# Another order for the start of a Fourier-and-maxout kernel: transfers, weight conversions and early quads

## The chip, the cores and the metric

The kernel runs on one core of a Trainium2 chip. The metric is the device time of one execution in microseconds (us). Engines are named as in the profile: PE does the matmuls, DVE, ACT and POOL work on tiles, SP here only issues DMAs; ACT and POOL issue some as well.

## What is computed

x has the shape (8, 3072, 256), in float32. The reference, cut to what matters:

```python
X = np.fft.rfft(x, axis=1)
Yr = Xr @ w_r - Xi @ w_i + b_r
Yi = Xr @ w_i + Xi @ w_r + b_i
Yr = np.sign(Yr) * np.maximum(np.abs(Yr) - lam, 0.0)     # lam = 0.01, Yi likewise
y = np.fft.irfft(Y, n=3072, axis=1)
h = np.maximum(np.maximum(y @ w1, y @ w2), y @ w3)       # 24576 rows, 256 to 768
out = h @ w_out                                          # 768 to 256
```

The expert weights w1, w2, w3 and w_out arrive in float64.

## The kernel before

**The Fourier part** of one batch has two levels, because 3072 = 96 x 32. *Stage a* is a 96-point transform as matmuls into `pa`; it goes over 8 quads, each of 4 of the 32 columns. A quad loads x (`load_x`), takes the largest magnitudes `mxx` that later set the scale (batch 1 on), copies `pa` to `aq` on ACT (L465) and writes it to the DRAM tile `a_d` (L466). Then come 12 *groups*: a group k reads its rows `aj` of `a_d`, does the 64-point blocks into `px` (L524, tables `mb_f`), the products with w_r, w_i into `py` (L551, L552, weights `wst`), adds the bias (`uf`, L555), thresholds (ACT L557 and L558, DVE L559), takes the maximum `mxu` (L712) and goes back through `pz` (L567; the last group L570, table `qf`). ACT copies `pz` to `zs` (L731) and writes it to the DRAM tile `z_d` (L732). Batch 0 does this in plain float32, stage a of batch 1 too; later batches split every operand into two parts and use three matmuls (`mm3`, L159 to L161).

**The expert part** loops over batch b, chunk c (8 of 384 rows) and f (6 slices of 128 of the 768 columns): `load_z` reads `zq` from `z_d`, `split_z` makes `zh` on ACT and `zl` on DVE (L153, L154), `inverse` transforms into `pi` and splits to `yh`, `yl`; `up` does the three products `pu`, with their maximum on DVE (`c` L817, `h` L820); `down` does `pd`. Stage a and the groups of the next batches are woven in between by a list of `events`, each with a position in units of f.

**The prologue** is batch 0's Fourier part; no expert work runs beside it. Its loop (L911) runs k from -3 to 12 and hands out loads and weight work by `plan[k]`. With k=12 done, two quads of batch 1 run their stage a, then 16 matmuls on a tile of zeros (`idle_matmuls`, L867), then `load_z`, `split_z`, `inverse` and the first `up`. I call this stretch, from the last `pz` to the first `pu`, the *pause*: PE has to wait there for z_d to go to DRAM and back. There are 9 idle matmuls at the very start and 32 between stage a and the groups.

**The weights.** `Weights` converts a float64 block of 384 columns (up) or 256 (down) into two float16 parts with integer work on DVE and ACT, in three steps: `exponent` (DVE L352, ACT L355), `combine` (DVE L359, L362, L366, L367) and `finish` (ACT L126, DVE L127, L373); `largest` (L328) takes the maximum first. There are 12 up blocks and 6 down blocks. Six and three go through the groups by the plan; the rest are `units`, of which each call of `pump` moves every running one a step on and begins another. The maxima of w_r, w_i and of the bias (`mxc`, `mxb` L289), their exponents (a transposing matmul `pt`, L237) and the float16 parts of w_r and w_i come in `split_fft_weights`, called at b=c=0, f=2.

**What sets the order.** A scheduler orders the instructions of each engine; `issue_after` puts an instruction behind another in that order without a wait on the chip. Each engine issues its own DMAs in its own order. SP loads x, the tables, w_r, w_i, `aj`, the expert weights and `zq`; ACT writes `z_d`, and `a_d` from batch 1 on; POOL loads `qf`, the bias (`bias`, and one row of 1 KB more into partition 96, L225), the identity and `bias_ri`, and writes the eight quads of batch 0 to `a_d`.

Of the kernel before, what the change touches and what calls it, by code (L numbers as in the profile page):

```python
# [93 lines left out]
def fourier_maxout_kernel(  # L94
    ctx: ExitStack, tc: tile.TileContext, x, w_r, w_i, b_r, b_i, w1, w2, w3, w_out, fa, ga, mb, mq, ident, out
):
    nc = tc.nc
# [11 lines left out]
    NATIVE = 2 * NCH  # L109

# [35 lines left out]

    def split_later(hi, lo, src, scale=None):
        h = hi if hi.dtype == F16 else hi.bitcast(F32)
        if scale is None:
            nc.scalar.activation(out=hi, in_=src, func=AF.Copy)  # L150
            later(lambda: nc.vector.tensor_tensor(out=lo, in0=src, in1=h, op=ALU.subtract))
        else:
            nc.scalar.activation(out=hi, in_=src, func=AF.Copy, scale=scale)  # L153
            later(lambda: nc.vector.scalar_tensor_tensor(  # L154
                out=lo, in0=src, scalar=scale, in1=h, op0=ALU.mult, op1=ALU.subtract
            ))
# [44 lines left out]
    def x_tile(name):  # L201
        return fft.tile([P, 2 * D], F32, name=name, bufs=2)
# [9 lines left out]
    def load_fft_weights():  # L212
# [12 lines left out]
        nc.gpsimd.dma_start(out=bias[96:97, 1, :], in_=rows[0])  # L225
        return [ws[:, kd] for kd in range(KD)]

# [21 lines left out]
    def power(name, e, sign, add, bufs=3):  # L249
# [3 lines left out]
        nc.vector.tensor_scalar(out=t, in0=t, scalar1=23, scalar2=None, op0=ALU.logical_shift_left)  # L253
# [14 lines left out]
    def split_fft_weights(ws):  # L268
# [7 lines left out]
        sc = power("sc", e, -1.0, 267.0, 1)  # L276
# [10 lines left out]
        split_scaled(*(t.rearrange("p a b -> p (a b)") for t in (qh, ql, qf)), Q_SCALE)  # L287
# [11 lines left out]


# [6 lines left out]
    class Weights:  # L307
        def __init__(self, name, parts, both):
            self.name, self.parts, self.raw, self.both = name, parts, {}, both
            self.mx = fft.tile([P, len(parts)], F32, name="mw" + name, bufs=1)  # L310


        def load(self, n, homes=None):
            src = [self.parts[n + i][2] for i in range(2)]
            width = src[0].shape[1]
            if homes:
                for i, t in enumerate(homes):
                    raw = t.rearrange("p j d -> p (j d)").bitcast(U32)[:, 0:width]
                    nc.sync.dma_start(out=raw, in_=src[i])
                    self.raw[n + i] = raw.rearrange("p (v w) -> p v w", w=2)  # L320
                return
            raw = raw_tile("rw").bitcast(U32)[:, 0:2 * width].rearrange("p (k c) -> p k c", k=2)
            nc.sync.dma_start(out=raw, in_=self.both(n))
            for i in range(2):
                self.raw[n + i] = raw[:, i].rearrange("p (v w) -> p v w", w=2)

        def largest(self, n):
            nc.vector.tensor_reduce(  # L328
                out=self.mx[:, n:n + 1], in_=self.raw[n][:, :, 1].bitcast(F32), axis=AX.X, op=ALU.max,
                apply_absolute_value=True,  # L330
            )
# [9 lines left out]
        def phases(self, n):  # L341
            hi, lo, _ = self.parts[n]
            raw = self.raw[n]
            width = raw.shape[1]
            lw, hw = raw[:, :, 0], raw[:, :, 1]
# [3 lines left out]
            def exponent():  # L349
                e = x_tile("xh").bitcast(U32)[:, 0:width]  # L350
                t["g"] = g = x_tile("xl").bitcast(U32)[:, 0:width]
                nc.vector.tensor_scalar(  # L352
                    out=e, in0=hw, scalar1=0x7FF00000, scalar2=None, op0=ALU.bitwise_and
                )
                nc.scalar.activation(out=g, in_=e, func=AF.Relu, scale=8.0, bias=ebias)  # L355
# [27 lines left out]
        (wuh[:, i, kd, v:v + HALF], wul[:, i, kd, v:v + HALF],  # L383
         up_v[i][kd * P:(kd + 1) * P, 2 * v:2 * v + 2 * HALF])
        for v in range(0, FF, HALF) for i in range(3) for kd in range(KD)
    ], lambda n: up_v[n % 6 // 2][:, n // 6 * 2 * HALF:(n // 6 + 1) * 2 * HALF].rearrange(
        "(k p) w -> p k w", p=P
    ))
    w_dn = Weights("d", [
        (woh[:, f], wol[:, f], out_v2[f * P:(f + 1) * P]) for f in range(NF)  # L390
    ], lambda n: out_v2[n * P:(n + 2) * P].rearrange("(k p) w -> p k w", p=P))
# [19 lines left out]

    def batch(b, kind):
# [13 lines left out]
    def load_x(q):  # L426
        b, q4 = divmod(q, NCH)
        xv = x[b].rearrange("(n1 n2) d -> n1 n2 d", n2=N2)[:, q4 * NQ:(q4 + 1) * NQ, :]
        with tc.issue_after(st["ld"].ins) if q >= NCH + 2 else nullcontext():
            if 2 <= q < NCH:  # L430
# [6 lines left out]

    def split_x(q):
# [79 lines left out]
    def first_b(k):  # L518
# [17 lines left out]
        if k == NJP - 1:  # L536
            st["ts"] = s_tile("tsf").rearrange("p (h m) -> p h m", h=KD)
            nc.gpsimd.tensor_copy(out=st["ts"], in_=t[:, :, 192:320])
# [178 lines left out]
    def stage_q(k):  # L717
# [13 lines left out]
        nc.scalar.activation(out=zs, in_=pv, func=AF.Copy, scale=st[b, "sv"][1] if b else 1.0)  # L731
# [6 lines left out]
    events = []  # L738

    def at(pos, fn, i, k=None, n=None):  # L740
        if n is None or 0 <= k < n:
            events.append((pos, len(events), fn, i))

    for q in range(NCH + 2, NB * NCH):
# [15 lines left out]
    events.sort(key=lambda e: e[0:2])  # L760
# [98 lines left out]
    def load_first_blocks(i):  # L859
        k = slice(6 * i, 6 * i + 6)  # L860
        nc.sync.dma_start(out=mb_f[:, k], in_=mq[:, 2 + 6 * i:8 + 6 * i])
# [14 lines left out]
    load_first_blocks(0)  # L876
    fft_weights = load_fft_weights()
# [3 lines left out]
    idle_matmuls(32)  # L881
    nc.gpsimd.dma_start(out=id_sb, in_=ident)
# [21 lines left out]
    for n in range(6):  # L904
        planned((4, 4, 5, 5, 7, 7)[n], w_dn.largest, n)
    planned(7, w_dn.scale)
    for n in range(3):
        planned(5 + n, prepare, w_dn, n)
        planned(8 + n, phase, w_dn, n)

    for k in range(-3, NJP + 1):  # L911
# [108 lines left out]
```

## Time and profile before

| | |
|---|---|
| median of three runs | 2042.45 us (2041.36 to 2044.1) |
| profiled execution | 2041.44 us, of which the span of the trace is 2039.6 us |
| granted TensorE clock, mean | 0.998 |
| PE, DVE, ACT busy | 99%, 71%, 51% of the span |
| first `px` of group 0 | at 31.90 us |
| last `pz` of group 11 | at 101.39 us |
| first `pu` | at 112.68 us |

A row of a timeline gives the start, the duration, the engine with its line and the tiles (out<-in), and in brackets how long the engine had been idle and what released it. In a row of grouped instructions stand the count, the busy time and the mean in ns. A row of windows gives the busy time of PE, PE's weight loads, DVE, ACT and POOL, then the granted clock, the DMA engines' busy share and GB/s.

### The profile page before, as it was taken

The page shows a single profiled execution, that of the slowest core. Times are in us where ns is not written, and L with a number is a line of the kernel's source. Part 1 is how long each engine was busy: PE and PEld are TensorE (multiplying, and loading weights), DVE is VectorE, ACT ScalarE, POOL GpSimd, SP SyncE. Part 2 cuts the span into 40 slices and gives each one's busy share as a digit, 9 for nine tenths or more (in the row PEclk, how much of TensorE's full clock was granted, in tenths as well). Part 3 has the DMA queues.
Part 4 walks back from the last instruction along what each step waited for, and adds up shares of the span by engine and source line. Part 5 has one row for each costly group of instructions (what it writes and reads, how often), then busy time and mean ns, then how long its engine had stood idle before and what let it go on. Part 6 is the DMA issues. An engine that isn't in the chain of part 4 may idle for free.

```text
span 2039.6 us, 40089 instructions
## 1 busy us (share of the span) xinstructions
PE 2016.9 (99%) x15836; PEld 1413.9 (69%) x15836; DVE 1447.3 (71%) x2813; ACT 1032.3 (51%) x2050; POOL 24.3 (1%) x81
## 2 busy tenths in 40 slices
PE   8999999999999999999999999999999999999999
PEld 4756776677776777677776777767777677776666
DVE  3997886678766877668776777767876677755544
ACT  4756554455544554445554555545554455533333
POOL 1000000000000000000000000000000000000000
PEclk9999999999999999999999999999999999999999
DMA  9455542434333442434434344243441423211100
GB/s 312 149 160 140 141 119 86 119 99 124 93 103 84 120 115 72 125 80 123 105 95 113 81 120 104 80 117 98 109 111 47 117 73 100 66 53 32 40 24 24
DMA packets 199535, 207.74 MB, mean 102 GB/s; under 512 B 20131, under 2 KB 177827, under 8 KB 199251
## 3 DMA queue, kind: packets, MB, share of 16 engines
q1 hardware_dynamic: 138371, 129.20, 24.8%
q10 hardware_dynamic: 59744, 72.11, 11.1%
q0 software_dynamic: 1232, 3.87, 0.6%
q8 instruction: 124, 2.03, 0.4%
q14 instruction: 64, 0.52, 0.1%
HBM read 87.40 MB, written 75.50 MB: 80 GB/s over the span
## 4 chain that ended last, share of the span: by engine, by line
PE 89%; DMA 4%; DVE 4%; ACT 1%; issue 1%; SPq 0%; ACTq 0%; DVEq 0%
PE pu L159 17%; PE pu L160 17%; PE pu L161 17%; PE pd L161 6%; PE pd L160 6%; PE pd L159 6%; PE py L159 3%; PE py L161 3%; PE py L160 3%; PE px L586 2%; DMA ab<-a_d 1%; PE pa L161 1%; PE pa L160 1%; PE pa L159 1%; DMA zq<-z_d 1%; PE pi L161 1%
## 5 line engine op out<-in xcount | busy, mean ns | idle before, releaser
L159 PE MATMUL pu<-yh,wuh 128*128 128x384 f16 x2304 | 751.1, 326 | 6.0 <-ACT c L814 3.2
L160 PE MATMUL pu<-yl,wuh 128*128 128x384 f16 x2304 | 750.6, 326 | 0.9 <-DVE yl L154 0.7
L161 PE MATMUL pu<-yh,wul 128*128 128x384 f16 x2304 | 750.7, 326 | 0.0
L153 ACT ACTIVATE hh<-h 128x384 f16<-128x384 f32 x384 | 200.4, 522 | 530.8 <-DVE h L820 529.1
L817 DVE TENSOR_TENSOR c<-pu,c 128x384 f32<-128x384 f32 x384 | 211.9, 552 | 180.5 <-ACT c L814 93.7
L161 PEld LDWEIGHTS <-wul 128*128 128x128 f16 x2304 | 225.2, 98 | 150.9 <-issue 2.0
L159 PEld LDWEIGHTS <-wuh 128*128 128x128 f16 x2304 | 225.4, 98 | 130.5 <-issue 11.7
L160 PEld LDWEIGHTS <-wuh 128*128 128x128 f16 x2304 | 225.5, 98 | 130.0 <-issue 11.5
L161 PE MATMUL pd<-woh,hh 128*128 128x256 f16 x1152 | 313.7, 273 | 0.2 <-DVE ebf L294 0.2
L160 PE MATMUL pd<-wol,hh 128*128 128x256 f16 x1152 | 313.9, 273 | 0.0
L159 PE MATMUL pd<-woh,hh 128*128 128x256 f16 x1152 | 313.9, 273 | 0.0
L154 DVE SCALAR_TENSOR_TENSOR hh<-h,hh 128x384 f16<-128x384 f32 x384 | 213.1, 555 | 122.1 <-ACT hh L153 121.7
L814 ACT ACTIVATE c<-pu 128x384 f32<-128x384 f32 x384 | 185.8, 484 | 142.2 <-PE pu L161 123.4
L820 DVE TENSOR_TENSOR h<-pu,c 128x384 f32<-128x384 f32 x384 | 212.3, 553 | 57.9 <-PE pu L161 50.6
L159 PE MATMUL py<-wch,tt 128*128 128x256 f16 x504 | 137.4, 273 | 0.0
L161 PE MATMUL py<-wch,tt 128*128 128x256 f16 x504 | 137.3, 273 | 0.0
L160 PE MATMUL py<-wcl,tt 128*128 128x256 f16 x504 | 137.3, 272 | 0.0
L160 PEld LDWEIGHTS <-hh 128*128 128x128 f16 x1152 | 112.7, 98 | 33.4
L159 PEld LDWEIGHTS <-hh 128*128 128x128 f16 x1152 | 112.7, 98 | 33.4
L849 ACT ACTIVATE o<-pd,s1u 128x256 f32<-128x256 f32 x191 | 82.6, 466 | 82.2 <-PE pd L161 41.0
L161 PEld LDWEIGHTS <-hh 128*128 128x128 f16 x1152 | 112.7, 98 | 13.6 <-DVE ebf L294 0.5
L154 DVE SCALAR_TENSOR_TENSOR zl<-zq,s0u,zh 96x1024 f16<-96x1024 f32 (+1 forms) x65 | 81.9, 1262 | 31.8 <-ACT zh L153 31.8
(204 smaller groups left out, 2686.9 us busy)
## 6 DMA issues: line engine op xcount, KB each, us to landing
z_d<-zs ACTq DMA_DIRECT2D x96, 256.0 KB, 2.2
out_dram<-o ACTq DMA_DIRECT2D x190, 128.0 KB, 2.1
zq<-z_d SPq DMA_DIRECT2D x63, 384.0 KB, 4.1
xq<-in_x_dram SPq DMA_DIRECT2D x58, 384.0 KB, 4.1
a_d<-aq ACTq DMA_DIRECT2D x56, 384.0 KB, 3.3
ab<-a_d SPq DMA_DIRECT2D x84, 256.0 KB, 3.9
ab<-ab SPq DMA_DIRECT2D x336, 64.0 KB, 2.1
vb<-vb SPq DMA_DIRECT2D x308, 64.0 KB, 2.4
```

The source lines that it names most:

```text
L153: nc.scalar.activation(out=hi, in_=src, func=AF.Copy, scale=scale)
L154: later(lambda: nc.vector.scalar_tensor_tensor(out=lo, in0=src, scalar=scale, in1=h, op0=ALU.mult, op1=ALU.subtract))
L159: nc.tensor.matmul(o, lh, rh, start=start, stop=False, **kw)
L160: nc.tensor.matmul(o, lh, rl, start=False, stop=False, **kw)
L161: st["mm"] = nc.tensor.matmul(o, ll, rh, start=False, stop=stop, **kw)
L586: nc.tensor.matmul(pv[:, h, :, g // 2, g % 2], ah[:, g // 2, g % 2, h * P:(h + 1) * P], mb_sb[:, i, 4 * kb + g].rearrange("p (c m) -> p c ...
L814: nc.scalar.activation(out=c1, in_=p, func=AF.Copy)
L817: nc.vector.tensor_tensor(out=c1, in0=p, in1=c1, op=ALU.max)
L820: nc.vector.tensor_tensor(out=h32, in0=p, in1=st["c1"], op=ALU.max)
L849: nc.scalar.activation(out=o, in_=pd[t], func=AF.Copy, scale=st[b, "su"][1])
```

## The change

1. **Transfers.** POOL no longer loads `qf`, the bias and the identity ahead of the `a_d` writes: SP does, behind the first two `aj`, w_r and w_i. Only the 1 KB row is still POOL's, behind the writes, and `bias_ri` comes late. Of the first table block only a third is loaded ahead of `aj`, and the rest follows in pieces of 4 and 6. w_r and w_i are asked for in the loop at k=-3, and the expert weights one group later.
2. **Conversions.** Two up blocks (768 columns) or two down blocks (512) go through one instruction, apart from the down blocks 2 and 3. `exponent` works in place in one tile `xhl`.
3. **Held back.** From k=11 on, `pump` runs as `pumps`, behind `quiet`: first the power s1u of batch 0 on DVE and the last `zs` on ACT, later the last low part `zl` or `yl` on DVE. The x maxima of the early quads come later, by events.
4. **Early quads.** Five quads of batch 1 (8 to 12) run stage a in the pause instead of two. Their x is loaded at k=7 to 11, three of them into weight tiles. The idle matmuls become 34 (from 32) and 4 (from 16).
5. **Scales.** `scale_fft_weights` holds the maxima and exponents of w_r, w_i and the bias and runs at k=0; `split_fft_weights` keeps the rest, at f=2.

```diff
+    EARLY = NCH + 5
...
-        rows = [b.rearrange("(o d) -> o d", o=1) for b in (b_r, b_i)]
-        nc.gpsimd.dma_start(out=qf, in_=mq[:, 0:2])
-        for j in range(2):
-            for c in range(2):
-                nc.gpsimd.dma_start(
-                    out=bias[64 * c:64 * c + 64, j, :], in_=rows[c].broadcast_to([64, D])
-                )
-        nc.gpsimd.dma_start(out=bias[96:97, 1, :], in_=rows[0])
         return [ws[:, kd] for kd in range(KD)]
+
+    def load_tables():
+        rows = [b.rearrange("(r o d) -> r o d", r=1, o=1) for b in (b_r, b_i)]
+        for c in range(2):
+            nc.sync.dma_start(out=bias[64 * c:64 * c + 64], in_=rows[c].broadcast_to([64, 2, D]))
+        nc.gpsimd.dma_start(out=bias[96:97, 1:2], in_=rows[0])
+        nc.sync.dma_start(out=qf, in_=mq[:, 0:2])
+        nc.sync.dma_start(out=id_sb, in_=ident)
...
-            if 2 <= q < NCH:
+            if 2 <= q < NCH or NCH + 2 <= q < EARLY:
                 xq = raw_tile("xr")[0:N1, 0:NQ * D]
...
+    def largest_x(q, i, xp):
+        b, q4 = divmod(q, NCH)
+        with tc.issue_after(quiet[0]) if q < EARLY else nullcontext():
+            nc.vector.tensor_reduce(
...
+            if q >= EARLY:
+                largest_x(q, i, xp)
+            elif b:
+                at(1 + q4 / 2, lambda u: largest_x(*u), (q, i, xp))
...
-    idle_matmuls(32)
-    nc.gpsimd.dma_start(out=id_sb, in_=ident)
+    idle_matmuls(34)
...
-    for n in range(12):
-        if n % 2 == 0:
-            planned(-3 + n // 2, w_up.load, n)
+    for n in range(0, 12, 2):
+        planned(-2 + n // 2, w_up.load, n)
         planned(-2 + n // 2, w_up.largest, n)
-    for n in range(6):
-        planned(-1 + n, prepare, w_up, n)
+    for n in range(0, 6, 2):
+        planned(n, prepare, w_up, n)
         planned(5 + n // 2, phase, w_up, n)
...
         with tc.issue_after(st["ld"].ins):
+            if k == -3:
+                fft_weights = load_fft_weights()
+                load_first_blocks(2, 4)
+            if k == -2:
+                load_tables()
+            if k == 0:
+                scale_fft_weights(fft_weights)
...
-            if k in (7, 8):
+            if 7 <= k < 12:
                 load_x(NCH + k - 7)
             if k == 9:
-                units += [(w_up, n) for n in range(6, 12)] + [(w_dn, n) for n in range(3, 6)]
-            if k >= 9:
+                units += [(w_up, n) for n in (6, 8, 10)] + [(w_dn, n) for n in (3, 4)]
+            if k in (9, 10):
                 pump()
-    for q in (NCH, NCH + 1):
...
+    quiet = st["power"].ins, st["zs"].ins
+
+    def pumps(n):
+        with tc.issue_after(quiet[0]), tc.issue_after(quiet[1]):
+            for _ in range(n):
+                pump()
+
+    pumps(1)
+    for q in range(NCH, EARLY):
         split_x(q)
         stage_a(q)
-    idle_matmuls(16)
+    idle_matmuls(4)
...
+    quiet = st["low"].ins, st["zs"].ins
...
-                    for _ in range(5):
-                        pump()
+                    pumps(5)
                     if f == 2:
-                        split_fft_weights(fft_weights)
+                        with tc.issue_after(quiet[0]):
+                            split_fft_weights(fft_weights)
```

Where the order moves, at three places. First POOL at the start of the kernel, before:

```order
L219 DMA qf<-in_dft_ib_dram 128x256
L222 DMA bias<-in_b_r_dram 64x256
L222 DMA bias<-in_b_i_dram 64x256
L222 DMA bias<-in_b_r_dram 64x256
L222 DMA bias<-in_b_i_dram 64x256
L882 DMA id_sb<-in_ident_dram 128x128
L930 DMA bias_ri<-in_b_r_dram 128x256
L930 DMA bias_ri<-in_b_i_dram 128x256
L225 DMA bias<-in_b_r_dram 1x16x16
L466 DMA a_d<-aq 96x1024 x2
```

and after, where the eight quads lie in the tiles aq, zq, ga_sb and wuh, which are free at that time:

```order
L488 DMA a_d<-aq 96x1024 x2
L488 DMA a_d<-zq 96x1024
L488 DMA a_d<-ga_sb 96x1024 x3
L488 DMA a_d<-wuh 96x1024 x2
L228 DMA bias<-in_b_r_dram 1x16x16
L560 COPY tsf<-tf 128x256
L959 DMA bias_ri<-in_b_r_dram 128x256
```

Nine small loads stood ahead of the first a_d write; now none does, and the 1 KB row (1x16x16) stands behind the last.

Second, ACT in the pause, from the last `zs` on, before:

```order
L465 ACTIVATE aq<-pa 96x512
L466 DMA a_d<-aq 96x1024
L465 ACTIVATE aq<-pa 96x512
L126 ACTIVATE wuh<-rw,swu 128x384
L466 DMA a_d<-aq 96x1024
L355 ACTIVATE xl<-xh,ebias 128x384
L153 ACTIVATE zh<-zq,s0u 96x512 x2
L355 ACTIVATE xl<-xh,ebias 128x384
L153 ACTIVATE yh<-pi 128x384 x2
```

and after, where the first `aq` x2 is a half of each of the quads 8 and 9, and the others are both halves of one quad, 10, 11 and 12:

```order
L487 ACTIVATE aq<-pa 96x512 x2
L488 DMA a_d<-aq 96x1024 x2
L487 ACTIVATE aq<-pa 96x512 x2
L361 ACTIVATE xhl<-xhl,ebias 128x768
L488 DMA a_d<-aq 96x1024
L487 ACTIVATE aq<-pa 96x512 x2
L157 ACTIVATE zh<-zq,s0u 96x512
L488 DMA a_d<-aq 96x1024
L487 ACTIVATE aq<-pa 96x512 x2
L157 ACTIVATE zh<-zq,s0u 96x512
L488 DMA a_d<-aq 96x1024
L157 ACTIVATE yh<-pi 128x384 x2
```

Both halves of `zh` stood together behind two quads; now each half stands behind one or two quads more.

Third, DVE at the start of the groups, after (before, `mxc` and `mxb` stood ahead of all groups and their exponents `ec`, `eb` in the stretch from the pause to f=2):

```order
L277 TENSOR_REDUCE mxc<-wst 128x1 x2
L239 TENSOR_REDUCE col<-mxc 128x1
L128 SCALAR_TENSOR_TENSOR ql<-qf,qh 128x256
L577 TENSOR_TENSOR uf<-py,bias 128x512
L246 TENSOR_REDUCE ec<-pt 128x1
L284 TENSOR_REDUCE mxb<-bias 128x1
L247 TENSOR_SCALAR ec<-ec 128x1
L239 TENSOR_REDUCE col<-mxb 128x1
L250 TENSOR_SCALAR ec<-ec 128x1
```

`mxb`, which needs all of the bias with its 1 KB row, now stands behind the first `uf` and ahead of all later ones.

More of the change, by code (lines that the diff above doesn't have):

```diff
@@ L275, in split_fft_weights @@
         st["lim", "x"] = limits("x", e, 142.0)
-        sc = power("sc", e, -1.0, 267.0, 1)
+        st["sc"] = power("sc", e, -1.0, 267.0, 1)
+        mb = small("mxb")
+        nc.vector.tensor_reduce(
+            out=mb, in_=bias.rearrange("p j d -> p (j d)"), axis=AX.X, op=ALU.max,
+            apply_absolute_value=True,
+        )
+        st["eb"] = small("ebf")
+        nc.vector.tensor_scalar(
+            out=st["eb"], in0=exponent_of(mb, "b", 23, 0xFF, 60.0), scalar1=1.0, scalar2=-37.0,
+            op0=ALU.mult, op1=ALU.add,
+        )
+    def split_fft_weights(ws):
+        sc = st["sc"]
         for kd, t in enumerate(ws):
@@ L307, in fourier_maxout_kernel, with __init__ @@
     class Weights:
-        def __init__(self, name, parts, both):
-            self.name, self.parts, self.raw, self.both = name, parts, {}, both
+        def __init__(self, name, parts):
+            self.name, self.parts, self.raw = name, parts, {}
             self.mx = fft.tile([P, len(parts)], F32, name="mw" + name, bufs=1)
         def load(self, n, homes=None):
-            src = [self.parts[n + i][2] for i in range(2)]
-            width = src[0].shape[1]
+            width = 2 * self.parts[n][0].shape[1]
             if homes:
@@ L341, in phases @@
         def phases(self, n):
-            hi, lo, _ = self.parts[n]
             raw = self.raw[n]
-            width = raw.shape[1]
-            lw, hw = raw[:, :, 0], raw[:, :, 1]
+            pair, width = raw.shape[1:3]
+            if pair == 2:
+                hi, lo = self.parts[n][4]
+            else:
+                hi, lo = (t.rearrange("p (k c) -> p k c", k=1) for t in self.parts[n][0:2])
+            lw, hw = raw[:, :, :, 0], raw[:, :, :, 1]
             m, r = hw.bitcast(F32), lw.bitcast(F32)
@@ L349, in exponent @@
             def exponent():
-                e = x_tile("xh").bitcast(U32)[:, 0:width]
-                t["g"] = g = x_tile("xl").bitcast(U32)[:, 0:width]
+                g = x_tile().rearrange("p a b -> p (a b)")[:, 0:pair * width].bitcast(U32)
+                t["g"] = g = g.rearrange("p (k v) -> p k v", k=pair)
                 nc.vector.tensor_scalar(
-                    out=e, in0=hw, scalar1=0x7FF00000, scalar2=None, op0=ALU.bitwise_and
+                    out=g, in0=hw, scalar1=0x7FF00000, scalar2=None, op0=ALU.bitwise_and
                 )
-                nc.scalar.activation(out=g, in_=e, func=AF.Relu, scale=8.0, bias=ebias)
+                nc.scalar.activation(out=g, in_=g, func=AF.Relu, scale=8.0, bias=ebias)
             def combine():
@@ L436, in load_x @@
         st["x", q] = pairs
+    def largest_x(q, i, xp):
+        b, q4 = divmod(q, NCH)
+        with tc.issue_after(quiet[0]) if q < EARLY else nullcontext():
+            nc.vector.tensor_reduce(
+                out=batch(b, "x")[0:N1, 2 * q4 + i:2 * q4 + i + 1], in_=xp, axis=AX.X,
+                op=ALU.max, apply_absolute_value=True,
+            )
     def split_x(q):
@@ L537, in first_b @@
             st["ts"] = s_tile("tsf").rearrange("p (h m) -> p h m", h=KD)
-            nc.gpsimd.tensor_copy(out=st["ts"], in_=t[:, :, 192:320])
+            st["late"] = nc.gpsimd.tensor_copy(out=st["ts"], in_=t[:, :, 192:320])
             for z in (32, 96):
@@ L730, in stage_q @@
         zs = fft.tile([P, 2, D], F32, name="zs")
-        nc.scalar.activation(out=zs, in_=pv, func=AF.Copy, scale=st[b, "sv"][1] if b else 1.0)
+        st["zs"] = nc.scalar.activation(
+            out=zs, in_=pv, func=AF.Copy, scale=st[b, "sv"][1] if b else 1.0
+        )
         nc.scalar.dma_start(out=rows_of(b, "z", kb), in_=zs)
@@ L736, in stage_q @@
             st[b, "su"] = power("s0u", e, -1.0, 261.0), power("s1u", e, 1.0, add)
[L738 to L744, printed above, removed]
+    for q in range(EARLY, NB * NCH):
         b, i = divmod(q, NCH)
```

104 lines of the change are left out of this document (50 added, 54 removed).

## The prediction

> **What bounds the kernel now.** I read the page's totals first, then the PE timeline of the first 155 us, then the chain of waits in order of time, and last the timelines of POOL, DVE and ACT and the DMA issues.
>
> ```profile
> span 2039.6 us, 40089 instructions
> PE 2016.9 (99%) x15836; PEld 1413.9 (69%) x15836; DVE 1447.3 (71%) x2813; ACT 1032.3 (51%) x2050; POOL 24.3 (1%) x81
> ```
>
> PE fills 99% of the span, so the only time to be had lies where PE waits or runs the idle matmuls, which compute nothing. PE's timeline shows these places (start, duration; in brackets the idle time before and its releaser):
>
> ```profile
> 10.58 2.31 PE L462 MATMUL pa<-xr,fr 96*96 96x512 f32 x5
> 14.40 7.41 PE L462 MATMUL pa<-xr,fr 96*96 96x512 f32 x16 [1.51 <-DMA xr<-in_x_dram]
> 21.65 7.07 PE L870 MATMUL idle<-zeros 128*128 128x512 f16 x32
> 31.90 1.13 PE L524 MATMUL px<-mb_all,aj 128*128 128x128 f32 x8 [3.18 <-DMA aj<-a_d]
> ...
> 101.39 1.35 PE L570 MATMUL pz<-uf,qf 128*128 128x256 f32 x4 [1.66 <-DVE uf L559]
> 112.68 0.65 PE L159 MATMUL pu<-yh,wuh 128*128 128x384 f16 x3 [0.41 <-ACT yh L153]
> 153.66 0.33 PE L159 MATMUL pu<-yh,wuh 128*128 128x384 f16 x1
> ```
>
> I cut the start at these moments. px of group 0 starts at 31.90; E = 102.74 is the end of the last pz (101.39 and 1.35); P = 112.68 is the first pu; S = 153.66 is the first pu of chunk 1, f=2. From S on, PE's list is the same in both kernels, and up to S it has the same pu, pd and pa, so the change is worth what it moves S. The three pieces are 70.84 (group stage), 9.94 (pause) and 40.98 (first chunk).
>
> **The front, up to px of group 0.** The chain gives the last a_d write and the read behind it, and PE's pieces of the first groups; the POOL rows show who held the writes; the count of packets by queue from 15 to 17 us has SP's queue, q1, alone; the DMA issues up to 140 us give KB and median time to landing:
>
> ```profile
> 22.73 6.22 DMA a_d<-wuh
> 28.97 2.80 DMA aj<-a_d
> ...
> 34.79 0.85 PE py L552 x2
> 36.50 1.34 PE px L524 x8
> 37.84 0.43 PE py L552 x2
> 41.29 0.89 PE px L524 x8
> ```
> ```profile
> 11.96 0.52 POOL L225 DMA_DIRECT2D bias<-in_b_r_dram  x1 [6.19 <-DMA bias<-in_b_i_dram]
> 12.47 1.03 POOL L466 DMA_DIRECT2D a_d<-aq  x2
> ```
> ```profile
> q1 hardware_dynamic: 141, 0.48, 103.4%
> ```
> ```profile
> z_d<-zs ACTq DMA_DIRECT2D x12, 256.0 KB, 2.2
> ...
> a_d<-aq ACTq DMA_DIRECT2D x4, 384.0 KB, 3.8
> ...
> bias<-in_b_r_dram POOLq DMA_DIRECT2D x1, 1.0 KB, 7.7
> ```
>
> Before, POOL stood 6.19 us for its bias loads ahead of the a_d writes, and wst and the table blocks shared q1 with x. After, the writes stand first on POOL and x has q1 nearly alone. I let PE's 1.51 wait for x go (bounds 0 and 1.51), so the last a_d write is issued near 21.1 in place of 22.73. It no longer has a backlog of seven writes ahead, so I price it at the 3.8 us of the four later a_d writes; the other end is the 6.22 of its own row. aj is then asked for at 25.0 instead of 28.97 and px starts at 27.9: **-4.0** (bounds -1.5 and -4.6). The 34 idle matmuls, at 7.07/32 = 0.22 each, reach from 20.2 to 27.7 and cover the wait, so the 3.18 us hole closes as well.
>
> **The group stage, 70.84.** Step by step:
> - Behind the 3.18 us hole, the py pairs cost 1.08, 0.85 and 0.85 against 0.43, and px 1.34 against 0.89: a half-speed stretch of 0.65+0.42+0.42+0.45 = 1.9. Its clock stands in the window below (0.77 over 35 to 40). Without the hole: **-1.9** (bounds 0 and -1.9).
> - Two pt matmuls (the exponents of wst and bias), which ran in the pause, now run between py of groups 0 and 1. A pt pair on PE costs 0.44 to 0.68 by its rows below: **+0.55**.
> - Three pa matmuls instead of two stand ahead of the last pz, at 1.71/2 = 0.86 each: **+0.86**. They and a lighter DVE list cover most of the 1.66 wait for uf: **-1.35** (bounds -0.86 and -1.66).
> - The bias maximum mxb now stands early in DVE's list, between uf of group 0 and everything behind it, and PE's second pt waits for it. It needs the 1 KB row that POOL sends, which waits in turn for the bias loads that SP now issues behind aj, wst, a table block and a second aj, some 1.5 MB. At the 396 GB/s of the window from 35 to 40 below that is 3.8 us from 25.0, and with some 2.5 us until the last is through (an aj read alone took 2.80) they land near 31.3. Before, this row took 7.7 us (issue 11.96, mxb at 19.69) beside a full q1. PE reaches that pt at about 36.0 (first py at 29.75, 12 py at 0.43, px 0.89, pt 0.22). A row that lands at once costs nothing; one that takes 7.7 lands at 39.0 and holds PE until mxb's 0.69 and a column copy are through, 3.9. I take **+2.5**, nearer to the row. A half-speed stretch behind that wait (0 to 1.9) I leave out of the sum and keep in the range.
>
> ```profile
> 35.00:40.00 5.00, 5.00 (x23) 4.45 (x22) 3.46 (x9) 1.99 (x4) 0.00 (x0) 0.77 1.03 396
> ```
> ```profile
> 102.74 1.71 PE pa L462 x2
> 104.88 0.44 PE pt L237 x2
> ```
> ```profile
> 109.69 0.68 PE L237 MATMUL pt<-id_sb,col 128*128 128x128 f32 x4
> ```
> ```profile
> 19.69 0.69 DVE L289 TENSOR_REDUCE mxb<-bias 128x1 f32<-128x512 f32 x1 [11.60 <-DMA bias<-in_b_r_dram]
> ```
>
> The Trainium skill, "DMA: Bandwidth & Descriptors", section "Anatomy of one DMA — SWDGE (gpsimd) path", gives about 2.0 us fixed and little for 1 KB, and its section "Queues, rings and completion order" says that an engine takes its queues in turn, packet by packet. By that page the row would land near 33.3 and the +2.5 would be nothing. The 7.7 us row and the software queue without one packet from 15 to 17 speak against it.
>
> Sum of the stage: -1.9 + 0.55 + 0.86 - 1.35 + 2.5 = **+0.7**; E moves by -4.0 + 0.7 = -3.3.
>
> **The pause from E to P, 9.94.** Before, two quads of batch 1 had their stage a here and the chain ran over zs, its write, the read as zq, zh, zl, the inverse. After, five quads do. ACT is the engine to follow, because it copies pa into aq (two buffers), writes a_d and also makes zh:
>
> ```profile
> 103.41 0.37 ACTq L732 DMA_DIRECT2D z_d<-zs  x1
> 105.11 0.34 ACTq L466 DMA_DIRECT2D a_d<-aq  x1
> 107.12 0.66 ACT L126 ACTIVATE wuh<-rw,swu 128x384 f16<-128x384 f32 x1
> 108.75 1.32 ACT L153 ACTIVATE zh<-zq,s0u 96x512 f16<-96x512 f32 x2
> ```
> ```profile
> 110.29 1.41 DVE L154 SCALAR_TENSOR_TENSOR zl<-zq,s0u,zh 96x512 f16<-96x512 f32 x2
> ```
>
> In the new order of ACT, aq of the third quad stands ahead of the first zh, and aq of the fourth and fifth quads ahead of the first and second. Third and fourth wait for the first two buffers to be written out, the fifth for the third's write. From E: zs, a double-width wuh and two aq halves, 2.4; the write of the first quad, 3.8; two aq halves, 1.0; the write of the third, 3.8; two halves, 1.0; the second zh, 0.66; the second zl, 0.75; and from zl's end (111.70) to pu (112.68), 0.98. Sum 14.4: **+4.5**. Two a_d writes as quick as z_d's 2.2 would give 11.2, two like the 6.22 row 19.2; z's own path, at 9.94, is the floor. I take the 3.8 row, since it is the same transfer on the same queue. The conversions that DVE has ahead of zl, at the prices below 0.92 + 0.87 + 0.92 + 0.47 + 0.87 + 0.87 + 0.47 = 5.4 and with its scalar rows about 6.9, are done by E+7, in time; from there to E+13.4 DVE has only the two zl and stands about 5 us.
>
> **From P to S, 40.98.** Three quads' pa, six at 0.86, no longer stand here: -5.1. But DVE gets the conversions that were held back. One 768-wide conversion is priced from the 384- and 256-wide rows of 30 to 140 us (start to start 0.08 less than the mean):
>
> ```profile
> L127 DVE SCALAR_TENSOR_TENSOR rw<-rw,swu,wuh 128x384 f32<-128x384 f32 x12 | 7.2, 611 | 0.0
> ...
> L359 DVE SCALAR_TENSOR_TENSOR xl<-rw,xl 128x384 uint32<-128x384 uint32 x12 | 6.5, 551 | 0.4 <-ACT xl L355 0.4
> ...
> L127 DVE SCALAR_TENSOR_TENSOR rw<-rw,swd,woh 128x256 f32<-128x256 f32 x4 | 1.9, 477 | 0.0
> ...
> L359 DVE SCALAR_TENSOR_TENSOR xl<-rw,xl 128x256 uint32<-128x256 uint32 x4 | 1.7, 416 | 0.0
> ...
> L362 DVE TENSOR_SCALAR rw<-rw 128x384 uint32<-128x384 uint32 x12 | 4.2, 353 | 0.0
> ```
> ```profile
> 125.00:130.00 5.00, 5.00 (x38) 3.37 (x36) 5.00 (x22) 1.32 (x3) 0.00 (x0) 1.00 0.15 48
> ```
> ```profile
> 143.76 0.54 DVE L820 TENSOR_TENSOR h<-pu,c 128x384 f32<-128x384 f32 x1
> ```
>
> From 256 to 384 wide the L359 form grows by 0.135; three such steps more make 768 wide 0.47 + 0.40 = 0.87, against two of 384 at 0.94: pairing saves 8%. In the same way L127 gives 0.92, and L362, growing by 0.07, 0.47. DVE was full beside PE here (5.00 of 5 from 125 to 130). Adding up DVE's new list from P at these prices puts the last h of f=5 at P+34.4; before it ended at 144.2, P+31.5. So DVE is 2.9 later while PE has 5.1 less to do. Laid against PE's list, PE stands 2.0 at the pu of f=3, 2.8 at the pd behind f=1, and 0.55, 1.3 and 0.55 behind: 7.2 of waits, where the old list by the same count has 1.2. So +6.0 - 5.1 = **+0.9** (bounds -6.3, no wait at all, and +2.9, DVE's whole delay). Of the 16 idle matmuls of the pause 4 are left, and PE may enter f=0 at half speed, 1.9 at most as above; I cost that at nothing, as DVE is behind PE there, and at 1.9 if it is not.
>
> **Sum.** -4.0 + 0.7 + 4.5 + 0.9 = +2.1. Against the profiled execution's 2041.44 (span 2039.6 and 1.84 around it) that is 2043.5; the three runs' median, 2042.45, is 1.0 above it, so I forecast 2044.5 for the median. A change under 0.2%, 4.1 us, cannot be told from none by this measurement: faster means below 2038.4, slower above 2046.5.
>
> **The rivals.**
> - *DVE keeps up after P.* If pairing and holding back leave DVE less to do than my widened prices say, PE's waits don't grow and all of the 5.1 comes: P to S 6.0 better than forecast, 2038.5. For it: the 5 us in which DVE stands in the longer pause. Against it: the 5.00 of 5 row, and the conversions have not become fewer elements. If the 1 KB row comes at once too, 2036.0.
> - *The bias row is late.* It lands at 39.0 or later, as the 7.7 row says; PE waits 3.9 and a half-speed stretch of 1.9 follows, as after the hole of 3.18. That is 1.4 + 1.9 more: 2047.8. It decides from about 38 us on, when the wait is over twice the 1.66 us one. For it: DMA at 1.03 of 16 engines. The Trainium skill's "TensorE: Matmul & The Clock Gate", section "What's actually happening", asks for an idle window of about 3.4 us before the clock halves; by it a wait of 2.5 would cost no clock. The window from 100 to 105 below, with only a 1.66 us wait behind it, is at 0.72 and speaks against that.
>
> ```profile
> 100.00:105.00 5.00, 3.61 (x9) 2.03 (x10) 4.19 (x9) 2.86 (x6) 0.00 (x0) 0.72 0.49 155
> ```
>
> - *The early start runs into the transfers.* wst, bias, qf, identity and table blocks, some 1.5 MB, now pass between 25 and 35 us, where 396 GB/s is what the engines give. If py of group 0 or px of group 1 waits for them, the 3.3 is lost: 2047.8. Against it: the expert weights come one group later, which frees that much.
>
> - *The bias row is served at once.* If queues are served in turn, the row lands before PE asks for it, the 2.5 goes, and the rest stands: 2042.0, no change. For it: z_d, on a third queue, has a median of 2.2 over the same stages. Against it: the 7.7 row. The rule quoted from the page above says the same.
>
> **How the numbers follow.** Forecast: 0.40. DVE keeps up: 0.23, of which half lies under 2038.4, and more with the row at once. Row at once alone: 0.13. Late row: 0.16. Transfers: 0.08. A little of the forecast's own spread (the pause at its ends, -3.2 and +4.8) falls to each side. That makes faster 0.22, same 0.51, slower 0.27. The range, 2036.5 to 2049.5, reaches from the first rival with the row at once to the late row with a slower a_d write; the forecast's own is 2040.5 to 2047.
>
> **What would show it.** Right: px of group 0 near 27.9 with under 1 us of waiting before it; py pairs at 0.43 from the start; a PE wait of 1 to 4 us at the second pt, released by DVE's mxb; ACT's second zh at E+12; P at E+14; DVE full until P+34 and PE waiting some 7 us between P and S. Wrong: px still past 30; an E-to-P of 10 (two aq buffers are not the chain) or over 17; S at P+36 with no waits (DVE keeps up); or a difference that arises after S, which I say holds none.

## The result and the profile after

The change made the kernel slower: 2056.1 us median of six runs (2052.16 to 2058.72) beside 2042.63 of the kernel before, ratio 1.0063, 95% interval 1.0045 to 1.0080. In a later set, beside three of the experiments below, it was 1.0042 (1.0029 to 1.0054). The forecast was +2.1 us; it is +13.5. The kernel before itself has medians of 2046.5 to 2047.9 in the sets of the experiments, so below times are compared by their ratios, and stages by the traces.

The profiled execution took 2058.15 us (span 2056.4). PE's timeline of it, at the places by which the prediction divided it:

```profile
19.09 7.50 PE L887 MATMUL idle<-zeros 128*128 128x512 f16 x34
27.05 1.13 PE L546 MATMUL px<-mb_all,aj 128*128 128x128 f32 x8 [0.46 <-DMA aj<-a_d]
...
31.28 1.13 PE L546 MATMUL px<-mb_all,aj 128*128 128x128 f32 x8 [1.28 <-DMA aj<-a_d]
...
41.69 0.49 PE L241 MATMUL pt<-id_sb,col 128*128 128x128 f32 x2 [4.69 <-DVE ec L250]
42.02 0.84 PE L573 MATMUL py<-wst,tf 128*128 128x256 f32 x2
42.65 1.06 PE L574 MATMUL py<-wst,tf 128*128 128x256 f32 x2
...
103.03 1.03 PE L592 MATMUL pz<-uf,qf 128*128 128x256 f32 x4
...
113.73 0.22 PE L163 MATMUL pi<-ga_sb,zh 96*128 96x96 f16 x1 [2.58 <-ACT zh L157]
...
119.34 0.26 PE L163 MATMUL pi<-ga_sb,zh 96*128 96x96 f16 x1 [4.01 <-ACT zh L157]
...
121.21 0.80 PE L163 MATMUL pu<-yh,wuh 128*128 128x384 f16 x2 [0.26 <-ACT yh L157]
...
134.67 0.32 PE L163 MATMUL pu<-yh,wuh 128*128 128x384 f16 x1 [1.84 <-DVE h L837]
...
139.98 0.28 PE L165 MATMUL pd<-woh,hh 128*128 128x256 f16 x1 [2.46 <-DVE hh L158]
...
167.03 0.33 PE L163 MATMUL pu<-yh,wuh 128*128 128x384 f16 x1
```

So E = 103.03 + 1.03 = 104.06, P = 121.21 and S = 167.03. The pieces, forecast and measured:

| piece | before | forecast | after | after less before |
|---|---|---|---|---|
| px of group 0 starts | 31.90 | 27.9 | 27.05 | -4.9 |
| groups, px to E | 70.84 | 71.5 | 77.01 | +6.2 |
| pause, E to P | 9.94 | 14.4 | 17.15 | +7.2 |
| P to S | 40.98 | 41.9 | 45.82 | +4.8 |
| S | 153.66 | 155.8 | 167.03 | +13.4 |

S moves by as much as the median. What follows S takes 1885.9 us in the trace of before (2039.6 - 153.66) and 1889.4 in this one; in all the traces below it lies between 1885.5 and 1889.9, whatever the variant, so I take the 3.5 of it for scatter of single executions.

In the groups, POOL's 1 KB row was issued at 34.84, when SP's bias loads had landed, and DVE's mxb came at 40.76. First POOL, then DVE:

```profile
20.17 0.51 POOL L488 DMA_DIRECT2D a_d<-wuh  x1 [1.21 <-ACT wuh L487]
34.84 0.49 POOL L228 DMA_DIRECT2D bias<-in_b_r_dram  x1 [14.16 <-DMA bias<-in_b_i_dram]
```
```profile
40.76 0.69 DVE L284 TENSOR_REDUCE mxb<-bias 128x1 f32<-128x512 f32 x1 [4.60 <-DMA bias<-in_b_r_dram]
```

The row's own time, among the DMA issues from 32 to 36 us:

```profile
bias<-in_b_r_dram POOLq DMA_DIRECT2D x1, 1.0 KB, 5.9
```

In the pause, ACT's timeline is the forecast chain, down to the order of its rows. The fifth quad's copy waits 3.93 us for the write that was issued at 111.23, which took until 117.60. That write itself left 0.7 us late, because it stands behind a conversion (L361) that waited for DVE:

```profile
109.38 1.08 ACT L487 ACTIVATE aq<-pa 96x512 f32<-96x512 f32 x2 [2.75 <-DMA a_d<-aq]
111.17 0.93 ACT L361 ACTIVATE xhl<-xhl,ebias 128x768 uint32<-128x768 uint32 x1 [0.71 <-DVE xhl L358]
111.23 0.31 ACTq L488 DMA_DIRECT2D a_d<-aq  x1
112.01 1.05 ACT L487 ACTIVATE aq<-pa 96x512 f32<-96x512 f32 x2
112.96 0.71 ACT L157 ACTIVATE zh<-zq,s0u 96x512 f16<-96x512 f32 x1
...
117.60 1.08 ACT L487 ACTIVATE aq<-pa 96x512 f32<-96x512 f32 x2 [3.93 <-DMA a_d<-aq]
118.57 0.72 ACT L157 ACTIVATE zh<-zq,s0u 96x512 f16<-96x512 f32 x1
```

The windows show two more things (busy PE, PE loads, DVE, ACT, POOL; then the granted clock): DVE was busy for only 2.16 of 5 us at the end of the groups, and full from 130 to 140; the clock was 0.58 in the window with P, and 0.62 and 0.69 in the ten us behind the second of PE's two long waits for DVE (1.84 and 2.46).

```profile
100.00:105.00 5.00, 4.26 (x14) 2.00 (x14) 2.16 (x6) 3.40 (x7) 0.00 (x0) 1.00 0.37 116
...
120.00:125.00 5.00, 4.62 (x23) 2.64 (x24) 3.03 (x6) 2.78 (x5) 0.00 (x0) 0.58 0.43 129
130.00:135.00 5.00, 3.16 (x25) 2.02 (x23) 5.00 (x12) 2.32 (x6) 0.00 (x0) 1.00 0.01 2
135.00:140.00 5.00, 2.40 (x16) 1.28 (x15) 5.00 (x11) 1.44 (x3) 0.00 (x0) 1.00 0.06 9
140.00:145.00 5.00, 4.64 (x16) 1.97 (x17) 4.29 (x10) 1.11 (x3) 0.00 (x0) 0.62 0.50 148
145.00:150.00 5.00, 5.00 (x19) 2.43 (x17) 2.79 (x7) 2.27 (x6) 0.00 (x0) 0.69 0.01 2
```

### The profile page after: what moved, and what is told of

Read it like the earlier page. It is cut to its first block, busy times and chain, and to the rows that moved or that the text cites. A ratio compares the mean times of both kernels' runs of the same rounds, so it can differ in the third digit from the quotient of the medians.

```text
span 2056.4 us, 39982 instructions
## 1 busy us (share of the span) xinstructions
PE 2017.9 (98%) x15826; PEld 1414.4 (69%) x15826; DVE 1444.3 (70%) x2749; ACT 1029.2 (50%) x2034; POOL 20.6 (1%) x75
## 4 chain that ended last, share of the span: by engine, by line
PE 90%; DMA 5%; DVE 2%; ACT 1%; issue 1%; SPq 1%; ACTq 0%; DVEq 0%; POOLq 0%
PE pu L163 17%; PE pu L164 17%; PE pu L165 17%; PE pd L164 6%; PE pd L163 6%; PE pd L165 6%; PE py L163 3%; PE py L164 3%; PE py L165 3%; PE px L608 2%; DMA zq<-z_d 1%; PE pa L163 1%; PE pa L165 1%; PE pa L164 1%; DMA ab<-a_d 1%; PE pi L165 1%
## 5 line engine op out<-in xcount | busy, mean ns | idle before, releaser
L163 PE MATMUL pu<-yh,wuh 128*128 128x384 f16 x2304 | 752.3, 327 | 11.3 <-DVE h L837 4.2
L165 PEld LDWEIGHTS <-wul 128*128 128x128 f16 x2304 | 225.5, 98 | 150.5 <-issue 1.8
```

What stands on the lines that cost most here:

```text
L163: nc.tensor.matmul(o, lh, rh, start=start, stop=False, **kw)
L165: st["mm"] = nc.tensor.matmul(o, ll, rh, start=False, stop=stop, **kw)
```

## The experiments

The theory after this trace: three costs of the change, each at its own place: the 1 KB row (groups), two aq buffers for five quads (pause), and the conversions that are held back (P to S). The rivals: late expert weights in the groups; the transfers beside the pause; and a chunk that is slow because of PE's clock or x and not because of DVE.

All traces in one table; E is the last `pz` with its 1.03 to 1.35, and S is taken 10.70 ahead of the first `pi` of the inverse for chunk 2, its distance in before (164.36 - 153.66) and after (177.74 - 167.03 = 10.71).

| kernel | px | groups | pause | P to S | S | ratio to before (95%) |
|---|---|---|---|---|---|---|
| before | 31.90 | 70.8 | 9.9 | 41.0 | 153.7 | 1 |
| changed | 27.05 | 77.0 | 17.2 | 45.8 | 167.0 | 1.0063 (1.0045, 1.0080) |
| changed, again | 27.55 | 77.7 | 17.7 | 43.7 | 166.5 | 1.0042 (1.0029, 1.0054) |
| row free | 26.88 | 73.7 | 17.2 | 44.1 | 161.9 | 1.0021 (1.0013, 1.0030) |
| three aq buffers | 27.33 | 76.6 | 13.5 | 43.4 | 160.8 | 1.0014 (1.0005, 1.0023) |
| two quads | 27.06 | 76.5 | 12.0 | 48.0 | 163.6 | 1.0022 (1.0013, 1.0031) |
| not held back | 26.52 | 77.4 | 16.1 | 36.8 | 156.8 | 1.0002 (0.9993, 1.0011) |
| tables late | 27.54 | 74.8 | 13.8 | 45.8 | 161.9 | 1.0023 (1.0014, 1.0032) |
| row free, w_r and w_i early | 27.07 | 70.2 | 17.1 | 44.1 | 158.4 | 1.0023 (1.0012, 1.0034) |
| two quads, row free, not held | 27.02 | 72.7 | 10.8 | 41.7 | 152.1 | 0.9983 (0.9973, 0.9993) |
| row free, three aq, not held | 27.20 | 73.9 | 10.9 | 39.2 | 151.1 | 0.9974 (0.9963, 0.9984) |
| the same, tables late | 27.00 | 74.7 | 10.9 | 37.9 | 150.5 | 0.9962 (0.9948, 0.9976) |
| the same, w_r and w_i early | 26.86 | 70.8 | 12.8 | 37.3 | 147.7 | 0.9952 (0.9939, 0.9965) |
| the same, 20 idle matmuls | 27.42 | 70.0 | 12.2 | 38.0 | 147.6 | 0.9966 (0.9954, 0.9978) |

Three things go with this table. The two traces of the changed kernel differ by 0.7 in the groups and by 2.1 from P to S, so a difference of that size between two single traces shows nothing by itself. S of before comes from its only trace, of an execution of 2041.44 us; its medians in the sets of the experiments are 4 to 5 us longer, and no trace shows where, so S and the ratio do not match line by line. And two matmuls of pa more (0.9 us) than in the changed kernel stand ahead of the last pz in "not held back", in "row free, three aq, not held" and in the row below it, and two fewer in both rows with two quads: that much shifts between groups and pause.

**The bias row free.**

```diff
-            nc.sync.dma_start(out=bias[64 * c:64 * c + 64], in_=rows[c].broadcast_to([64, 2, D]))
+            if c == 0:
+                nc.sync.dma_start(out=bias[0:64], in_=rows[c].broadcast_to([64, 2, D]))
+                continue
+            nc.sync.dma_start(out=bias[64:128, 0:1], in_=rows[c].broadcast_to([64, 1, D]))
+            nc.sync.dma_start(out=bias[64:96, 1:2], in_=rows[c].broadcast_to([32, 1, D]))
+            nc.sync.dma_start(out=bias[97:128, 1:2], in_=rows[c].broadcast_to([31, 1, D]))
```

> The bias load into partitions 64 to 127 is cut so that it leaves out the 1 KB row of partition 96; POOL can then send that row at the start, ahead of the a_d writes. Theory (PE's 4.69 us wait at the second pt, for mxb, and the half-speed stretch behind it come from that row alone): the wait is gone, px of group 0 to the end of the last pz falls from 76.8 to 70.5-72, the time to about 2050. Rival (the expert weights, asked for one group later, make DVE late in the groups): the wait moves to a later place, the stage stays above 75 and the time above 2054.

Half of it came: PE's wait at the second pt is gone, and the groups take 73.7 instead of 77.0, not 70.5 to 72. It isn't the rival's later wait for the weights either; what is left is a wait for the second aj with a stretch of low clock behind it:

```profile
31.22 1.92 PE L551 MATMUL px<-mb_all,aj 128*128 128x128 f32 x8 [1.39 <-DMA aj<-a_d]
```
```profile
30.00:35.00 5.00, 3.78 (x14) 3.42 (x15) 1.73 (x5) 1.18 (x3) 0.00 (x0) 0.66 0.92 295
```

**w_r and w_i ahead of the first aj**, with the row free, to test that.

```diff
     load_first_blocks(0, 2)
+    fft_weights = load_fft_weights()
...
             if k == -3:
-                fft_weights = load_fft_weights()
                 load_first_blocks(2, 4)
```

> The kernel with the bias row free, and w_r, w_i (512 KB) asked for behind x again, ahead of the first aj, instead of behind it. Theory (with the row free the groups still take 73.7 and not the forecast 69, because the second aj stands on SP's queue behind wst and a table block: a 1.4 us wait at the second px and a half-speed stretch behind it): that wait falls under 0.5, the clock from 30 to 35 us goes from 0.66 to 1.0, the groups take 71-72, the time is 2 us less than with the row free alone. Rival (wst then delays the a_d writes between 13 and 21 us, and px of group 0 starts later by as much): groups 71-72, but px at 28.5 or later, no gain.

The trace follows the theory: px stays at 27.07, the second px waits 0.58, the groups take 70.2 and S is 3.5 earlier. The ratio does not show it (1.0023 against 1.0021, intervals of 0.2%, measured in another set), so as a time this one is undecided; its window:

```profile
30.00:35.00 5.00, 4.65 (x23) 3.70 (x22) 1.72 (x5) 1.23 (x3) 0.00 (x0) 1.00 0.89 259
```

**Three aq buffers.**

```diff
-        return fft.tile([96, NQ * D], F32, name=name, bufs=1 if name == "zq" else 2)
+        return fft.tile([96, NQ * D], F32, name=name, bufs=1 if name == "zq" else 3)
```

> Three aq buffers instead of two, nothing else. Theory (the pause is ACT's chain: the fifth quad's copy waits for the write of the third quad, and the second zh stands behind it): that 3.93 us wait goes, the fifth quad waits only for the second quad's write, the pause falls from 17.3 to 11.5-13 us and the time to about 2051. Rival (the pause is as long as it is because of the transfers beside it, four table loads and the writes, or because of DVE's conversions): the pause stays above 15.5 and the time above 2054.

The pause falls to 13.5, above the theory's 11.5 to 13 and far below the rival's 15.5. ACT no longer waits for a write ahead of zh, but for DVE, whose held-back conversion ends at 111 (ACT's timeline):

```profile
106.97 1.27 ACT L487 ACTIVATE aq<-pa 96x512 f32<-96x512 f32 x2 [0.45 <-PE pa L484]
111.06 0.94 ACT L361 ACTIVATE xhl<-xhl,ebias 128x768 uint32<-128x768 uint32 x1 [2.83 <-DVE xhl L358]
...
113.84 0.71 ACT L157 ACTIVATE zh<-zq,s0u 96x512 f16<-96x512 f32 x1
```

**Two quads.**

```diff
-    EARLY = NCH + 5
+    EARLY = NCH + 2
...
-            if 7 <= k < 12:
+            if 7 <= k < 9:
...
-    idle_matmuls(4)
+    idle_matmuls(16)
```

> Only two quads of batch 1 in the pause, 16 idle matmuls behind them, all else as in the changed kernel. Theory: the pause falls from 17.3 to 10-11, as before the change; from the first pu to the first pu of chunk 1, f=2, the three quads' pa (5.1 us) come back but lie in PE's waits for DVE, so that this piece stays at 45-47; time about 2049-2050. Rival (the held-back conversions make the pause long): the pause stays above 14 and the time above 2053.

The pause falls to 12.0, not to 10 or 11, and P to S grows to 48.0: the three quads' pa do not lie in PE's waits, they cost 2.2 of their 5.1, or 4.3 beside the 43.7 of the changed kernel's second trace. S is 3.4 earlier than with five. The part of the pause that stays is ACT again: a half-ready conversion stands ahead of both zh and waits 4.07 for DVE:

```profile
110.29 0.98 ACT L127 ACTIVATE wuh<-rw,swu 128x768 f16<-128x768 f32 x1 [4.07 <-DVE rw L372]
111.18 0.92 ACT L361 ACTIVATE xhl<-xhl,ebias 128x768 uint32<-128x768 uint32 x1
112.00 1.32 ACT L157 ACTIVATE zh<-zq,s0u 96x512 f16<-96x512 f32 x2
```

**Conversions not held back.**

```diff
-        with tc.issue_after(quiet[0]), tc.issue_after(quiet[1]):
-            for _ in range(n):
-                pump()
+        for _ in range(n):
+            pump()
```

> The conversions are not held back any more (pumps without the two orderings; the x maxima still are). Theory (DVE has the work that was held back after the first pu, while it stood some 7 us in the pause): the piece from the first pu to the first pu of chunk 1, f=2 falls from 45.8 to 41-42, the pause stays at 17 since zl waits for zh there; time about 2052. Rival (that piece is long because PE starts it at half speed and waits for x of the next quads, not for DVE): it stays above 44.5 and the time above 2054.

P to S falls by 9.0, to 36.8, below the theory's 41 (by 6.9 beside the second trace of the changed kernel). About 6 of it are PE's waits, and the rest is the clock. DVE is full where it stood at the end of the groups, PE has none of its waits for h and hh left, and the clock stays at 1.00 where it had been 0.62:

```profile
100.00:105.00 5.00, 4.45 (x12) 1.82 (x12) 5.00 (x9) 4.00 (x8) 0.00 (x0) 1.00 0.41 123
130.00:135.00 5.00, 5.00 (x35) 3.23 (x33) 5.00 (x11) 1.54 (x3) 0.00 (x0) 1.00 0.40 89
135.00:140.00 5.00, 4.93 (x36) 3.06 (x34) 5.00 (x13) 2.88 (x6) 0.00 (x0) 1.00 0.21 70
140.00:145.00 5.00, 4.78 (x39) 2.50 (x38) 5.00 (x9) 2.38 (x5) 0.00 (x0) 1.00 0.51 147
```

This is the largest single part. It also brings the ratio back to 1.0002.

**The table loads behind the second zq.**

```diff
+        if (b, c) == (0, 1):
+            st["ld2"] = ld
...
-                        with tc.issue_after(st["ld"].ins):
+                        with tc.issue_after(st["ld2"].ins):
                             for i in (f - 3, f - 2):
```

> The four loads of batch 1's table blocks (384 KB each) stand behind the second zq load on SP instead of right behind the first; all else as in the changed kernel. Theory (the write of the third quad took 6.2 us and not 3.8 because these loads ran beside it): that write is back at 4 us or less, ACT's wait for it falls from 3.93 to 1.5-2, the pause from 17.3 to 15; time 2 us less than the changed kernel's. Rival (the write is slow by itself, as the 5.4 us median of two says): the pause stays at 17.

Confirmed, and larger than expected: the third quad's write is through 3.0 us after its issue, ACT's wait falls to 0.53, the pause to 13.8. (S is 5.1 earlier, of which 3.4 is the pause; the rest is the row, for which PE happened to wait 2.46 in this execution.) ACT and the DMA issues from 104 to 114:

```profile
109.47 0.32 ACTq L488 DMA_DIRECT2D a_d<-aq  x1
110.31 1.06 ACT L487 ACTIVATE aq<-pa 96x512 f32<-96x512 f32 x2
...
112.51 1.08 ACT L487 ACTIVATE aq<-pa 96x512 f32<-96x512 f32 x2 [0.53 <-DMA a_d<-aq]
```
```profile
a_d<-aq ACTq DMA_DIRECT2D x5, 384.0 KB, 3.0
```

**The changed kernel again**, beside the combinations:

> The changed kernel unaltered, to have it beside the others on one chip. All theories: px of group 0 at 27, 76-77 us of groups, a pause of 17 and 45-46 us to the first pu of chunk 1, f=2; 1.005 to 1.008 of the kernel before.

Px, groups and pause come within 0.7 of what was expected; P to S, 43.7, is lower, and the ratio, 1.0042, lies below the expected 1.005 to 1.008, with an interval that reaches into it. PE has the same two long waits for DVE as in the first trace, but this time the clock stays at 1.00 behind them. First PE's rows, then the windows:

```profile
136.50 0.32 PE L163 MATMUL pu<-yh,wuh 128*128 128x384 f16 x1 [1.84 <-DVE h L837]
...
141.81 0.28 PE L165 MATMUL pd<-woh,hh 128*128 128x256 f16 x1 [2.46 <-DVE hh L158]
```
```profile
140.00:145.00 5.00, 2.37 (x13) 1.34 (x14) 5.00 (x12) 0.52 (x1) 0.00 (x0) 1.00 0.40 94
145.00:150.00 5.00, 5.00 (x26) 2.61 (x25) 4.63 (x11) 3.23 (x7) 0.00 (x0) 1.00 0.36 107
```

**Row free, three aq buffers and nothing held back, together** (the three diffs above).

> The bias row free of the other bias loads and first on POOL, three aq buffers, and conversions not held back, together. Theory (three separate costs, which moved the first pu of chunk 1, f=2, by 5.1, 6.2 and 10.3 us one at a time): they add up to 21, that point comes at 145-147, some 7 us earlier than in the kernel before, and the ratio to it is 0.995 to 0.998. Rival (they cover one another: DVE's conversions have to be done somewhere, and without the waits in the groups and the pause they hold zl or the first h): that point stays at 151 or later and the ratio at 0.999 or above.

Between the two: S at 151.1 is where the rival had it, so 15.9 of the 21 adds up, and the ratio, 0.9974, is inside the theory's range, near its upper end. The pause is 10.9 where each single change left 13 and more; PE's waits for DVE behind P are back in part (0.79 for hh, 0.51 for c), probably since the conversions stand behind P again where the pause no longer gives them time; this was not tried.

**Two quads, row free, not held back.**

> The bias row free, conversions not held back, two quads in the pause and 16 idle matmuls behind them: of the change there remain the new order of the transfers, the pairing and the early scales. Theory: the groups take 73-74, the pause 10-12, the piece to the first pu of chunk 1, f=2, 40-42 (three quads' pa are back in it), that point comes at 151-153; ratio 0.998 to 1.000. If the five quads are worth having once their waits are gone, this one is slower than the one with all three by 4 us or more; the rival says that they are worth nothing and both are within 2 us.

As expected in every piece within 0.4 us, 0.9983. Five quads with their waits gone are 1.0 us ahead in S and 0.9 thousandths in the ratio, with intervals that overlap (0.9963 to 0.9984 and 0.9973 to 0.9993). The 4 us that would have shown their worth aren't there: they are worth at most little.

**Further on the best one**: the three together with the tables late, then with w_r and w_i early, then with 20 idle matmuls instead of 4.

> The three together (row free, three aq buffers, nothing held back) and the four table loads behind the second zq load. Theory (ACT's chain over aq still sets the pause, through the writes of the first two quads): the pause falls from 10.9 to 10 or a little less and the ratio to the kernel before to about 0.997. Rival (with three buffers the loads no longer matter): the same as without, within 1 us.

The pause did not change (10.9), so the rival's reason held for it; the ratio, 0.9962 in another set, can't be told from 0.9974.

> The same with w_r, w_i behind x. Theory: 1.5 to 2.5 us less than without; ratio about 0.996. Rival: px of group 0 later by as much, no gain.

S is 2.7 earlier, by 3.9 in the groups less 1.9 that come back in the pause; 2036.8 us beside 2046.52 of the kernel before, ratio 0.9952 (0.9939 to 0.9965): faster than the kernel before and the changed one. From the run without w_r and w_i early, 0.9962, the ratio can't be told.

> The same with 20 idle matmuls in the pause instead of 4. Theory (PE enters the expert part at half speed after the idle stretch of the pause, which cost some 1.4 us in the changed kernel): the first pu run at full speed, at most 1 us gained, since DVE is the later one there. Rival (idle matmuls stand in front of pi and delay it): a later first pu, 0 to 2 us lost.

No gain: P is 0.8 earlier, at full clock, and S the same within 0.1. Between P and S PE now waits 2.8 us, nearly all of it for DVE, where it waited 0.5, so the slow stretch at P had cost nothing: DVE was the later one. The window at P, without the idle matmuls and with them:

```profile
110.00:115.00 5.00, 4.74 (x19) 2.15 (x17) 3.54 (x7) 3.15 (x6) 0.00 (x0) 0.53 0.83 242
```
```profile
110.00:115.00 5.00, 4.37 (x27) 2.54 (x26) 4.33 (x9) 1.66 (x4) 0.00 (x0) 1.00 0.82 243
```

The rival's delay of the first pu isn't there. The time is 2.5 us longer than without the 16 matmuls (2039.34 and 2036.8), with intervals that overlap; in the traces the difference lies behind S (1889.9 and 1885.5), and its cause stays open.

## Why the prediction was wrong

Most places and causes were named rightly, and the sum was a sixth of the measured one, because four terms were too small or missing: the third quad's write, the row, the second aj, and the low clock behind PE's waits. Point by point:

- **The front, -4.0:** right, -4.9. The idle matmuls covered the wait for aj to 0.46, and the half-speed stretch of the first py is gone.
- **The row, +2.5:** the mechanism was right and the size short. PE waited 4.69; in the other executions with the row behind the bias loads 1.97 to 4.26. The bias loads ahead landed shortly before 34.8 and not at 31.3; the row itself took 5.9. The late-row rival had the row landing at 39.0 or later (it landed near 40.7) and the half-speed stretch behind it, 5.8 in all; 4.69 and some 1.8 were measured. In this trace the rival, and not the forecast, came true in the groups; the waits of the other executions lie on both sides of the forecast 2.5.
- **Transfers at nothing:** wrong. The second px waited 1.28 for its aj behind wst and a table block, and with the row away it brought a low-clock stretch in one trace: 3.5 us together (73.7 against 70.2). In three other traces with the row free the same wait, 1.14 to 1.71, left the clock at 1.00. The third rival named just this wait.
- **The pause, +4.5:** the chain over two aq buffers was right row by row. The step that failed is the price of the third quad's write: 3.8 was taken from writes of the earlier kernel, though the prediction's own order left four table loads behind zq on SP. It took 6.4 beside them, 6.9 in the second trace and 3.0 without (2.6 of the 2.75 us missing); the 6.22 row that the prediction had as its other end was the nearer one. By luck two smaller errors cancel: the first quad's write was back 0.9 earlier in the chain than forecast, and the third's left some 0.8 later behind its copies, held by the conversion that waited for DVE. The 17.15 lies just past the 17 that the prediction gave as a sign of being wrong.
- **P to S, +0.9:** the waits that the two lists gave came out: forecast 2.0, 2.8, 0.55, 1.3 and 0.55, measured 1.84, 2.46, 0.60, 0.40 and 0.41, with 0.36 for x: 6.1 in place of 7.2. What failed is that the sum had nothing for the clock in this piece. For the entry to f=0 it put it at nothing with a reason; for the stretch behind the waits it had no term. The windows lose 0.42 of 3.8 us behind P, 0.38 of 5 and 0.31 of 5: 1.6 + 1.9 + 1.55 = 5.05, which covers the 4.0 that were missing and the 1.1 by which the waits were less than forecast. This is a count of one trace and not a price: in the second trace PE waits the same 1.84 and 2.46, loses no clock behind them, and P to S takes 43.7, 1.8 above the forecast. And the reason given for f=0 held in the run with 20 idle matmuls, where full clock at P gained nothing; in the changed kernel DVE stood 0.85 us there for PE's first products. Nor was DVE full until P+34: between 144 and 150 it stood 2.9 us for ACT, whose parts of w_r and w_i come behind copies of pa, which PE did at low clock (0.4 us in the second trace).
- **DVE keeps up:** this rival needed the conversions where they had been. With them not held back P to S is 36.8, close to the 35.9 of this rival (41.9 less 6.0).
- **What follows S is the same:** right within the scatter.

In sum, 10.9 of the 11.3 us between forecast and trace are accounted for: the clock is about 5 in the chunk and some 1.8 in the groups, the table loads 2.6, the row 2.2 and the second aj 1.3; the front gave 0.9 back, and the waits in the chunk 1.1. That the groups' 1.8 is the clock is worked out from the py at 1.06 in the timeline and was not tried by itself. In the second trace the split is another (the windows lose about 1.7 in the chunk and 3.4 in the groups), and what decides whether a wait costs clock stays open. The parts of the change that were not undone alone are the pairing, the early scales and the expert weights one group later.

## What to carry to other kernels

Price each new wait on PE with a stretch of low clock behind it, as a range: behind the same two waits for DVE it cost some 3.4 us in one trace and nothing in the other. Work held back to keep an engine free for a later step costs whatever that engine then idles: DVE was busy for 2.16 of 5 us at the end of the groups, and 5.00 of 5 once the conversions were let run. And when a chain goes through a write, look at what the next queue issues at that moment, rather than at what the write took elsewhere.

## What the runs showed of the hardware

- The clock can fall behind short waits: to 0.66 in the window with the 1.39 us wait, to 0.62 and 0.69 behind waits of 1.84 and 2.46 that lay 2.9 us of work apart. The Trainium skill, "TensorE: Matmul & The Clock Gate", section "What's actually happening", asks for an idle window of about 3.4 us; these stretches followed shorter ones. It does not fall each time: it stayed at 1.00 behind the same 1.84 and 2.46 in the changed kernel's second trace, and behind a wait of 1.71 in the run with the three together.
- A 384 KB write from ACT's queue took 3.0 us with next to nothing on SP's queue (0.9% of 104 to 114) and 6.4 beside four 384 KB loads on it.
- The 1 KB row of POOL's queue took 5.9 us beside a full q1 (103% from 34 to 41) and 7.7 before. Of z_d's 256 KB writes on ACT's queue, two had a median of 6.4 beside q1 at 95% (before, 44 to 52), and one took 2.1 in the pause of the changed kernel.
